# Turning U and V by VectorE in 32x32 blocks instead of by TensorE

## The chip, the cores and the metric

The kernel runs on one core of one Trainium2 chip. The metric is the device time of one execution in microseconds (us). Engines are named as in the profile: PE is the matmul engine TensorE (PEld its weight loads), DVE is VectorE, ACT is ScalarE, POOL is GpSimd, SP is SyncE, which here only issues transfers. Each engine works through its own queue of instructions in order; PSUM is the memory that PE writes, in 8 banks.

## The reference

A sequence `x` of 2048 tokens of width 576 goes through two layers. Each layer is a Fourier mix with a residual, then a two-layer perceptron with a residual.

```python
def _A_ref(x, dft_seq_re, dft_seq_im, dft_hid_re, dft_hid_im):
    a = jnp.einsum("bsd,ed->bse", x, dft_hid_re)
    b = jnp.einsum("bsd,ed->bse", x, dft_hid_im)
    y = jnp.einsum("ts,bse->bte", dft_seq_re, a) - jnp.einsum("ts,bse->bte", dft_seq_im, b)
    return y
def _B_ref(x, w1, b1, w2, b2):
    y = _layernorm(x, axis=-1)
    h = _gelu(jnp.einsum("bsd,df->bsf", y, w1) + b1)
    return jnp.einsum("bsf,fd->bsd", h, w2) + b2

x = x + _A_ref(_layernorm(x), ...)
x = x + _B_ref(_layernorm(x), ...)
...
```

The two DFT matrices of the sequence are 2048x2048, the two of the width 576x576; `w1` is 576x4608 and `w2` is 4608x576. All of it is fp32.

## The kernel before, in words

The order of the Fourier mix is turned round: first the sequence product, then the hidden one. For each of the 16 tiles of 128 output tokens, the sequence product gives U = Cr z and V = -(Ci z), 128 x 1152 numbers (`uv`), where z is the normalized input. Then the hidden product multiplies U and V by the 1152 x 576 matrix `dh` (the real part above the imaginary part) and adds the result to the residual `X`.

Each fp32 operand of a matmul is split in two parts, a high half that PE's fp32r mode can hold (an ACT copy, `high`, or the first line of `split`) and the rest (a DVE subtraction, `low`, or the second line of `split`). Each product takes three passes (`PASSES`: high x high, high x low, low x high). Big products are done with seven multiplications instead of eight (`ORDER` names the seven), which costs sums and differences on DVE and POOL.

**The sequence product** (`Sequence.run`, lines 693 to 737). The first two tiles are plain products, done together in `first_mms`, input block by input block, in all 8 banks; `first_post` (599) copies each tile's four banks with ACT into a buffer and stores it to DRAM (`uv_mid`) from ACT's queue. The other 14 tiles are 7 steps each, 98 in all, of 24 matmuls. At step n the program emits, in this order: loads of blocks of the DFT matrix as ring buffers come free (`load_c`, on SP), the low half for step n+2 (DVE, with differences that belong to it), the sums of the next tile if the step is number 2 of `ORDER`, the high half for step n+3 (ACT), the 24 matmuls, and `post` (668), which takes the step's bank. The last of a tile's seven, i = 4, ends in line 689 (DVE) and the store of the tile from SP (690). In layer 0 each step also advances the background work (`pump`), which makes the split parts of `w1` with ACT, DVE and POOL. The program order on each engine is the order of emission: nothing is reordered by a scheduler.

Before the first of the 98 steps stands what is left of `Sequence.fill` (lines 477 to 484): the low half of step 0 with its sums, the high halves of steps 1 and 2, the sums of the last input block on DVE and POOL (`right_sums`), their high and low halves (`high_sums`, `low_sums`). `first_post(0)` is emitted ahead of these, `first_post(1)` after step 1.

**The hidden product** (`Hidden`, and `hidden` from 868). It is done in two halves of 8 tiles. A tile's U and V are loaded from DRAM (`load_uv`, 832) into one of two slots. `turn` (845) puts the transpose into PSUM, because PE contracts over partitions: 9 PE transposes of 128x128 into two pairs of banks taken from a ring of four (`space`), then three splits out of PSUM (512, 512 and 128 columns). In the loop over tiles (988 to 1026) the turn of tile n+1 is emitted ahead of the 54 matmuls of tile n. Tile 0 of the first half is turned in the last steps of the sequence product (`begin`, n == 5, line 772); tile 0 of the second half is turned in the last outer products of the first half's perceptron (`steps`, line 799).

**The perceptron** (`mlp`) follows each half. The change doesn't touch it.

## Time and profile before

| what | value |
|---|---|
| median of 3 runs | 2691.88 us (2689.53 to 2692.5) |
| span of the profiled execution | 2687.7 us |
| mean granted TensorE clock | 0.999 |
| sequence product, layer 0 | to about 375 us |
| hidden product, first half, layer 0 | about 375 to 440 us |
| hidden product, second half, layer 0 | from about 875 us |
| sequence product, layer 1 | about 1345 to 1720 us |
| hidden products, layer 1 | from about 1720 us, and from about 2204 us |

The profile is one execution of the program. Its span is the time from the first to the last instruction; the timed runs also hold what lies around it. A row of the timeline has the start, the length, the engine, the line of the program, the operation, output and input by the program's names, the count of merged instructions, and in square brackets the idle time of the engine before it with what ended that. A row of a group (lines by form) has the busy time, the mean length in ns, and the idle time before with its causes. Line 205, 195, 198 and 201 are helpers (matmul, add, subtract, split); a row there is told apart by its shape. In the rows of stretches, each engine's busy time stands in the order PE, PEld, DVE, ACT, POOL, then the granted clock and the share and rate of the transfers.

### The profile page before, as it was taken

What the parts mean: (1) busy time and instruction counts of PE and PEld (TensorE: products, weight loads), DVE (VectorE), ACT (ScalarE), POOL (GpSimd) and SP (SyncE); (2) the same over time, 40 slices, a digit from 0 to 9 for tenths busy, and PEclk for the clock granted to TensorE, in tenths of its full rate; (3) what the DMA queues carried; (4) which work ended last, traced back from release to release, by engine and by line L of the source; (5) the groups of instructions that cost most, each with busy time, mean ns of one, the idle gap of its engine ahead of it and who ended that gap; (6) DMA issues with size and microseconds to landing.
All of it is one profiled execution on the core that took longest, in us unless ns stands there. A gap on an engine that the chain in (4) does not pass through costs nothing. (4 is left out here: it accounts for less than half of the span.)

```text
span 2687.7 us, 45270 instructions
## 1 busy us (share of the span) xinstructions
PE 2663.8 (99%) x17540; PEld 2498.7 (93%) x17540; DVE 1770.9 (66%) x2575; ACT 1101.4 (41%) x1837; POOL 791.3 (29%) x738
## 2 busy tenths in 40 slices
PE   9999999999999999999999999999999999999999
PEld 9999999888888988988899999999989899899998
DVE  8888866877777565556676666466555546655555
ACT  6555545544443343333354333343333324433332
POOL 6322234444443432222250000142222234322222
PEclk9999999999999999999999999999999999999999
DMA  5777775777778466676553333546666673666664
GB/s 190 253 259 245 243 264 186 261 265 273 262 267 305 148 187 195 191 221 208 161 202 130 122 123 124 191 145 193 193 194 196 191 274 115 206 194 194 193 194 153
DMA packets 209286, 544.92 MB, mean 203 GB/s; under 512 B 22048, under 2 KB 56864, under 8 KB 208928
## 3 DMA queue, kind: packets, MB, share of 16 engines
q1 hardware_dynamic: 195744, 511.94, 58.8%
q10 hardware_dynamic: 13328, 30.09, 2.9%
q8 instruction: 139, 2.28, 0.3%
q14 instruction: 75, 0.61, 0.1%
HBM read 429.87 MB, written 114.72 MB: 203 GB/s over the span
## 5 line engine op out<-in xcount | busy, mean ns | idle before, releaser
L205 PE MATMUL bank<-R 128*128 128x288 f32 (+2 forms) x16972 | 2607.8, 315 | 14.5 <-DVE A L195 5.6
L205 PEld LDWEIGHTS bank<-R 128*128 128x128 f32 x16972 | 2437.4, 188 | 176.0 <-DVE A L195 18.0
L195 DVE TENSOR_TENSOR A<-bank,A 128x576 f32<-128x576 f32 (+3 forms) x808 | 568.5, 710 | 536.5 <-PE bank L205 454.8
L198 POOL TENSOR_TENSOR R<-A,R 128x512 fp32r<-128x512 f32 (+1 forms) x286 | 373.2, 1315 | 903.9 <-ACT R L1230 864.4
L198 DVE TENSOR_TENSOR R<-A,R 128x1024 fp32r<-128x1024 f32 (+9 forms) x523 | 496.1, 972 | 56.0 <-ACT R L643 22.4
L195 POOL TENSOR_TENSOR A<-A 128x576 f32<-128x576 f32 (+2 forms) x102 | 138.1, 1358 | 564.9 <-ACT A L683 366.1
L1169 ACT ACTIVATE bank<-bank,b1t 128x512 f32<-128x512 f32 (+1 forms) x224 | 144.9, 647 | 369.1 <-DVE bank L195 242.5
L1230 ACT ACTIVATE R<-A 128x512 fp32r<-128x512 f32 x288 | 176.8, 629 | 271.8 <-DVE A L198 123.5
L198 POOL TENSOR_TENSOR A<-A 128x384 f32<-128x384 f32 (+3 forms) x156 | 197.3, 1267 | 246.2 <-DVE R L198 118.7
L643 ACT ACTIVATE R<-A 128x1024 fp32r<-128x1024 f32 x196 | 204.6, 1052 | 121.2 <-DVE A L198 98.2
L195 DVE TENSOR_TENSOR bank<-bank,A 128x512 f32<-128x512 f32 (+1 forms) x228 | 152.3, 670 | 143.4 <-PE bank L205 142.6
L198 DVE TENSOR_TENSOR R<-bank,R 128x512 fp32r<-128x512 f32 (+1 forms) x328 | 205.3, 640 | 51.5 <-ACT R L201 46.8
L198 DVE TENSOR_TENSOR A<-A 128x1024 f32<-128x1024 f32 (+3 forms) x134 | 140.9, 1058 | 4.5 <-DVE R L198 0.2
L1196 ACT ACTIVATE A<-bank 128x512 f32<-128x512 f32 (+1 forms) x76 | 43.7, 576 | 225.8 <-PE bank L205 225.8
L1230 ACT ACTIVATE R<-bank 128x512 fp32r<-128x512 f32 x216 | 121.4, 595 | 30.3 <-PE bank L205 30.3
L198 DVE TENSOR_TENSOR A<-bank,A 128x512 f32<-128x512 f32 x144 | 98.1, 681 | 0.0
L201 ACT ACTIVATE R<-bank 128x512 fp32r<-128x512 f32 (+1 forms) x112 | 49.4, 490 | 81.4 <-PE bank L855 75.2
L1169 ACT ACTIVATE A<-bank,b1t 128x512 f32<-128x512 f32 (+1 forms) x76 | 50.6, 666 | 66.6 <-DVE bank L195 66.6
L685 DVE SCALAR_TENSOR_TENSOR A<-A 128x288 f32<-128x288 f32 x28 | 16.0, 572 | 83.4 <-POOL A L195 83.4
L275 ACT ACTIVATE R<-A 128x256 fp32r<-128x256 f32 x126 | 51.9, 412 | 41.8 <-DMA A<-in_w 17.8
L249 ACT ACTIVATE A<-A,moments 128x576 f32<-128x576 f32 x58 | 48.6, 863 | 48.2 <-POOL moments L230 19.8
L276 ACT ACTIVATE R<-A,power,middle 128x128 fp32r<-128x128 f32 x126 | 60.8, 483 | 0.0
(66 smaller groups left out, 625.9 us busy)
## 6 DMA issues: line engine op xcount, KB each, us to landing
R<-w_parts SPq DMA_DIRECT2D x504, 320.0 KB, 3.4
R<-w_parts SPq DMA_DIRECT2D x189, 576.0 KB, 3.7
A<-in_cs SPq DMA_DIRECT2D x112, 512.0 KB, 4.0
w_parts<-R SPq DMA_DIRECT2D x63, 576.0 KB, 4.8
w_parts<-R ACTq DMA_DIRECT2D x81, 320.0 KB, 3.0
uv_mid<-A SPq DMA_DIRECT2D x28, 576.0 KB, 3.1
w_parts<-R SPq DMA_DIRECT2D x45, 320.0 KB, 4.3
A<-in_w SPq DMA_DIRECT2D x72, 192.0 KB, 4.6
```

The source lines that it names most:

```text
L195: engine.tensor_tensor(dst, a, b, op=op)
L198: engine.tensor_tensor(dst, a, b, op=OP.subtract)
L201: nc.scalar.activation(hi, src, AF.Copy)
L205: nc.tensor.matmul(o, a, b, start=start, stop=stop, skip_group_check=True)
L249: nc.scalar.activation(dst, src, AF.Identity, bias=mv[:, 4:5], scale=mv[:, 3:4])
L275: nc.scalar.activation(t[:, 1:4:2], src[:, 0:3:2], AF.Copy)
L276: nc.scalar.activation(t[:, 2], src[:, 1], AF.Identity, bias=power[:, 2:3], scale=middle)
L643: nc.scalar.activation(self.cells[t, i](2, NP, P)[:, 0], self.source(t, i), AF.Copy)
L685: nc.vector.scalar_tensor_tensor(uv[:, 1, 0], p7, -1.0, u, op0=OP.mult, op1=OP.subtract)
L1169: nc.scalar.activation(dst, src, AF.Gelu_apprx_tanh, bias=bias(f))
L1196: nc.scalar.activation(up, o, AF.Copy)
L1230: nc.scalar.activation(H[q, k](2, TC)[:, 0], src, AF.Copy)
```

## The change

DVE transposes each finished tile of U and V in place, block by block of 32x32 (one instruction over 128 x 1152), before it is stored. A 32x32 block then holds 32 of the 1152 columns in its rows, but still in the partitions of its 32 tokens. The load from DRAM moves the blocks to partitions by column group: four transfers, one for each 32 partitions, each of 32 partitions x 4 runs of 288 numbers. What lies in SBUF is then the whole transpose, with the columns in another order: partition 32c + d, chunk k holds column 288c + 32k + d. The rows of `dh` are put into the same order on the host. `turn` is then one split, an ACT copy and a DVE subtraction over 128 x 1152 that read the loaded tile with runs of 32 numbers, and no PSUM is used for it; `space` is no longer called there, so the other users of the ring of banks get other banks.

```diff
+    def turned(block):
+        nc.vector.transpose(block(2 * D), block(2 * D))
...
                     nc.scalar.activation(uv[:, i, 1 - j], banks[4 * (1 - t) + 2 * i + j][:, :DH], AF.Copy,
                                          scale=-1.0 if i else 1.0)
+            turned(out)
             nc.scalar.dma_start(uvd[t], out(2 * D))
...
                 nc.vector.scalar_tensor_tensor(uv[:, 1, 1], b, -1.0, u, op0=OP.mult, op1=OP.subtract)
+                turned(self.out)
                 dma(uvd[t], self.out(2 * D))
...
             self.uv[n] = self.uvs.take()
-            at = self.uv[n](2 * D)
-            dma(at.bitcast(F32) if self.half else at, uvd[8 * self.half + self.order[n]])
+            at = self.uv[n](4, DH)
+            src = uvd[8 * self.half + self.order[n]].rearrange("(q d) (c k) -> c d q k", q=4, c=4)
+            for c in range(4):
+                to = at[32 * c:32 * c + 32]
+                dma(to.bitcast(F32) if self.half else to, src[c])
...
-            v = self.uv[n](KH, P)
-            v = v.bitcast(F32) if self.half else v
+            v = self.uv[n](2 * D)
+            v = (v.bitcast(F32) if self.half else v).rearrange("p (q k t) -> p k q t", q=4, t=32)
             self.ut[n] = place or R.place(UT_AT[self.half][n % 2], 2 * KH * P)
-            o = self.ut[n](2, KH, P)
-            a, b = self.space(), self.space()
-            for k in range(KH):
-                at = (a, b)[k // 8][:, k // 4 % 2, k % 4 * P:(k % 4 + 1) * P]
-                nc.tensor.transpose(at, v[:, k], ident)
-            for k0, k1, at in ((0, 4, a[:, 0]), (4, 8, a[:, 1]), (8, 9, b[:, 0, 0:P])):
-                split(o[:, 0, k0:k1], o[:, 1, k0:k1], at.rearrange("p (k t) -> p k t", t=P))
-                yield
+            o = self.ut[n](2, KH, 4, 32)
+            split(o[:, 0], o[:, 1], v)
+            yield
             self.uvs.give(self.uv.pop(n))
...
-    dh = np.concatenate([dr.T, di.T], axis=0).reshape(KH, P, D)
+    dh = np.concatenate([dr.T, di.T], axis=0).reshape(4, KH, 32, D).transpose(1, 0, 2, 3).reshape(KH, P, D)
```

## The prediction

> **What bounds the kernel now.** I read the page's busy table first, then TensorE's timeline for its idle places, the rows of the transposes and of the splits by form, the timeline of DVE, ACT and SP round each place that gets new work, and the table of stretches.

> ```profile
> span 2687.7 us, 45270 instructions
> PE 2663.8 (99%) x17540; PEld 2498.7 (93%) x17540; DVE 1770.9 (66%) x2575; ACT 1101.4 (41%) x1837; POOL 791.3 (29%) x738
> ```

> TensorE (PE) is busy for 99% of the span, so whatever leaves its stream shortens the kernel, as long as nothing that PE waits for becomes later. The two questions are how much PE time the transposes take, and where VectorE (DVE), which gets new work, is already close behind PE. The profiled execution's span is 2687.7 us. The median of the three timed runs is 2691.9, so 4.2 us lie around the span, and I leave them alone.

> **What is removed from PE.** Line 855 makes 9 transposes per tile for 32 tiles:

> ```profile
> L855 PE MATMUL bank<-ident,A x144: 270/272/328, 371.9 to 1772.2; 128*128 128x128 f32 x144
> L855 PE MATMUL bank<-ident,R x144: 270/273/327, 864.7 to 2254.0; 128*128 128x128 f32 x144
>   DVE A L195: 0.9, 4
> ...
> 377.06 2.92 PE L205 MATMUL bank<-R 128*128 128x288 f32 x20 [0.36 <-DVE R L198]
> 393.16 1.15 PE L855 MATMUL bank<-ident,A 128*128 128x128 f32 x9
> 394.06 7.44 PE L205 MATMUL bank<-R 128*128 128x288 f32 x54
> 864.68 1.15 PE L855 MATMUL bank<-ident,R 128*128 128x128 f32 x9
> 868.25 3.93 PE L205 MATMUL bank<-R 128*128 128x288 f32 x28 [0.80 <-DVE A L195]
> 2197.77 6.68 PE L205 MATMUL bank<-R 128*128 128x288 f32 x48 [0.71 <-DVE A L195]
> ```

> One transpose lasts 272 ns, but they are pipelined: nine start at 393.16 and the next matmul starts at 394.06. The price is therefore 0.90 us per tile, not 9 x 0.272, and 32 x 0.90 = 28.8 us leave the stream. Four groups of waits hang on them. The transposes themselves waited 0.9 us in all for PSUM banks that DVE had not freed. Tile 1 waited 0.36 us at 377.06 for its split, which came behind its transposes. At 868.25 and 2197.77 the first turn of the second half ran inside the last outer products: ACT and DVE could split only after PE's transposes, DVE's add to X was queued behind that, and PE waited for the bank (0.80 and 0.71). The new split depends on a load that is long home and uses no PSUM, so all four should go: 2.8 us. Removed: 31.6 us.

> **What changes in the splits.**

> ```profile
> L198 DVE TENSOR_TENSOR R<-bank,R 128x512 fp32r<-128x512 f32 x292 | 197.6, 683 | 51.5 <-ACT R L201 46.8 <-ACT R L1230 4.2
> L198 DVE TENSOR_TENSOR R<-bank,R 128x128 fp32r<-128x128 f32 x32 | 9.0, 281 | 0.0
> L201 ACT ACTIVATE R<-bank 128x512 fp32r<-128x512 f32 x76 | 43.0, 587 | 81.4 <-PE bank L855 75.2 <-issue 6.2
> L201 ACT ACTIVATE R<-bank 128x128 fp32r<-128x128 f32 x32 | 8.7, 272 | 0.0
> L198 DVE TENSOR_TENSOR R<-A,R 128x1152 fp32r<-128x1152 f32 x16 | 21.6, 1352 | 3.8 <-ACT R L579 3.8
> L579 ACT ACTIVATE R<-A 128x1152 fp32r<-128x1152 f32 x16 | 18.5, 1158 | 6.8 <-POOL A L198 6.8
> ```

> Per tile ACT had 2 x 587 + 272 = 1446 ns and gets one instruction of 1158. DVE had 2 x 683 + 281 = 1647 and gets 1352. Both lie beside 7.3 us of matmuls of the tile before, so I count nothing for them.

> **What is added to DVE.** One in-place transpose of 128x1152 fp32 per tile, 32 in all. No DVE transpose is in the trace. The nearest row has the same size and two operands, 1352 ns, and successive DVE instructions start about 0.09 us before the last one ends, so it costs the queue 1.27 us. I take that. [...]

> [...]

> **Where DVE has no room: the start of each layer's sequence product.** `first_post(0)` puts its transpose into DVE's queue ahead of the low half of the first step, and it waits for four copies out of PSUM, hence for PE.

> ```profile
> 59.66 0.41 ACT L603 ACTIVATE A<-bank 128x288 f32<-128x288 f32 x1 [0.38 <-PE bank L205]
> ...
> 58.77 1.22 DVE L195 TENSOR_TENSOR A<-A 128x1024 f32<-128x1024 f32 x1
> 60.03 3.15 DVE L198 TENSOR_TENSOR A<-A 128x1024 f32<-128x1024 f32 x3
> 63.64 1.58 DVE L198 TENSOR_TENSOR R<-A,R 128x1024 fp32r<-128x1024 f32 x1 [0.46 <-ACT R L643]
> 67.11 2.49 DVE L198 TENSOR_TENSOR R<-A,R 128x1152 fp32r<-128x1152 f32 x2 [1.89 <-ACT R L579]
> ...
> 69.66 19.34 PE L205 MATMUL bank<-R 128*128 128x288 f32 x144 [0.25 <-DVE R L198]
> 89.54 282.48 PE L205 MATMUL bank<-R 128*128 128x288 f32 x2134 [0.54 <-DVE R L198]
> ...
> 1404.32 0.41 ACT L603 ACTIVATE A<-bank 128x288 f32<-128x288 f32 x1 [0.38 <-PE bank L205]
> 1410.67 0.41 ACT L675 ACTIVATE A<-bank 128x288 f32<-128x288 f32 x1 [0.24 <-PE bank L205]
> ...
> 1401.16 1.22 DVE L195 TENSOR_TENSOR A<-A 128x1024 f32<-128x1024 f32 x1
> 1409.52 2.50 DVE L198 TENSOR_TENSOR R<-A,R 128x1152 fp32r<-128x1152 f32 x2 [1.90 <-ACT R L579]
> ```

> Before, DVE did the first low half early and began the sums at 58.77. With the change the last copy ends at 60.07, the transpose starts at about 60.1, the first low half (1.13) follows 1.27 later, and the sums begin at 62.5: the chain moves by 3.8 us. It is a chain: sums and differences on DVE, the right sums on POOL, ACT's high half, DVE's low sums and the low half of the third step, which ends at 69.60, just when PE, already 0.25 late, takes it. So the whole 3.8 us reach PE, most of it as a wait of about 2.8 in the second step (whose low half moves from 65.2 to 69.0, wanted at about 66.2). In layer 1 the copy ends at 1404.73 and the sums move from 1401.16 to 1407.2, by 6.0. The chain's end moves from 1412.02 to 1418.0. PE finished step 0 at 1410.6, so it wants it at 1410.6 + 3.2 + 0.3 = 1414.1: 4.0 us late. ACT's store of U and V also waits for the transpose; behind it stands a high half that waits longer anyway. `first_post(1)` has a 1.9 us gap in DVE behind it. Cost: 7.8 us.

> **The other 28 transposes.**

> ```profile
> 90.00:350.00 260.00, 260.00 (x1968) 260.00 (x1967) 224.71 (x247) 151.13 (x272) 79.29 (x53) 1.00 0.73 251
> 1425.00:1700.00 275.00, 275.00 (x2082) 275.00 (x2081) 181.54 (x189) 107.02 (x137) 9.67 (x12) 1.00 0.35 119
> ...
> 132.12 0.45 DVE L689 SCALAR_TENSOR_TENSOR A<-bank,A 128x288 f32<-128x288 f32 x1
> 134.66 1.92 DVE L198 TENSOR_TENSOR A<-A 128x1024 f32<-128x1024 f32 x1
> 142.42 1.23 DVE L195 TENSOR_TENSOR A<-A 128x1024 f32<-128x1024 f32 x1 [2.27 <-DMA A<-in_cs]
> 144.82 2.82 DVE L198 TENSOR_TENSOR R<-A,R 128x1024 fp32r<-128x1024 f32 x3
> ...
> 136.64 0.33 SPq L192 DMA_DIRECT2D A<-in_cs  x1
> ...
> 1436.13 0.46 DVE L195 TENSOR_TENSOR A<-bank,A 128x288 f32<-128x288 f32 x1 [2.33 <-PE bank L205]
> ```

> DVE is busy 86% of the stretch in layer 0 (it also makes the weight parts) and 66% in layer 1. A tile takes 7 x 3.17 = 22.2 us. In layer 0 that leaves 3.0 us, but not all of it is free. The transpose sits behind line 689; the subtraction of 134.66 follows it, frees a block, SP loads into it (136.64), and the sums at 142.42 wait for that load, so DVE's 2.27 us gap does not absorb a later transpose. The low half after those sums ends at 146.04; PE's step starts at 69.66 + 24 x 3.174 + 0.54 = 146.4 and takes it two matmuls later: 0.6 us to spare, 1.27 needed. The same reckoning for the other tiles of layer 0 (the last apart, whose low halves wait for ACT) gives 0.6 to 2.4 to spare, some 19 us over 12 tiles, and less than 1.27 in three (0.85, 0.6, 0.7): 1.7 us of waits. In layer 1 DVE waits 2.33 us for PE (1436.13) a few instructions behind line 689, before any load is wanted, and that gap takes the transpose in: nothing. SP's store waits for the transpose too, and the block load queued behind it is the one just counted.

> **The loads.**

> ```profile
> L192 SPq DMA_DIRECT2D A<-uv_mid x16: 319/325/2116, 355.7 to 1754.8; - x16
> DMA to landing us min/median/max: 2.8/3.7/8.7
> ```

> Four transfers instead of one: SP issues for 1.3 us instead of 0.33, and the slot is freed by DVE's split, not by PE. Loads are issued more than one tile (7.3 us) ahead of their split, and the split another ahead of the matmuls. Cover: matmuls of two tiles; nothing counted. Without it, 1 us per tile would be 32.

> **Sum.** 31.6 - 7.8 - 1.7 = 22.1 us: a span of 2665.6, and 2691.9 - 22.1 = **2669.8 us**.

> **Rivals.** *The transpose is dear* (the slower side). With a queue price T, the two starts cost 2T + 5.2 and layer 0, from about 2.4 us, 12T - 19: together 14T - 13.8. It decides from T = 3.2, where this equals 31.6. [...] 0.06. *Twice the price*: T = 2.6 costs 22.6 and leaves 9.0, so 2683. 0.10. [...] 0.12. *Late loads*: four small transfers per tile hold the split back by about a microsecond per tile, which gives it all back: about 2692. It speaks against it that landing took 3.7. 0.05. *Slow clock after the start waits*:

> ```profile
> 1328.77 6.92 PE L205 MATMUL bank<-R 128*128 128x288 f32 x48 [2.02 <-DVE A L195]
> ```

> PE's longest idle time is 2.02 us, and the granted clock in the stretches above is 1.00. My wait of 2.8 would be the longest yet; if PE then ran one step at half pace in each layer, 3.2 us more each, 2676. [...] 0.07.

> **Numbers.** My forecast has 0.60. The range of 2662 to 2684 runs from the cheaper transpose to twice the price and leaves out the dear transpose, the late loads and part of the cheaper case, under 2 in 10. Measurement tells about 0.2% (5.4 us) from no change. Faster: 0.60 + 0.10 + 0.12 + 0.07 = 0.89, less 0.01 that I give to same, with the late loads: 0.06; slower 0.06.

> **What the new profile would show.** Line 855 gone; 32 DVE transposes near 1.35 us; PE idle of about 4 us in all near 66 to 73 and again near 1400, released by DVE's low halves; a few waits under a microsecond up to 350; matmuls of one hidden tile following the last without a break. DVE transposes over 2.5 us, or PE waiting on the split while `uv_mid` lands, would make it wrong.

## The result, and the profile after

The changed kernel takes 2699.65 us (median of 6 runs, 2696.38 to 2701.92), the kernel before 2690.74 beside it (6 runs, 2689.48 to 2692.5): ratio 1.0032, 95% interval 1.0022 to 1.0042. It is slower by 0.3%. The forecast was 2669.8 with a range of 2662 to 2684; it is wrong in sign and by 30 us. The profiled execution of the changed kernel is the longest of its six (2701.92 us), that of the kernel before one of its shortest (2689.53), so the two spans below differ by 12.4 us where the medians differ by 8.9.

The busy table of the page after:

```profile
span 2700.1 us, 44682 instructions
PE 2647.4 (98%) x17252; PEld 2479.5 (92%) x17252; DVE 1812.7 (67%) x2543; ACT 1096.6 (41%) x1773; POOL 811.8 (30%) x738
```

PE's idle time is span less busy: 23.9 us before, 52.7 after. The record of the granted clock has, apart from one at the very end of each program, seven spells of 3.41 us at half speed after and none before. Half of each is lost, 7 x 1.705 = 11.9 us, and that hides in PE's busy time. PE's work at full clock is therefore 2647.4 - 11.9 = 2635.5, that is 28.3 less than before. So the account is -28.3 of work, +28.8 of waiting, +11.9 of half clock: +12.4 of span. The work went as forecast; the waiting ate it. Where it is, PE's waits after (total us, times, longest) say:

```profile
PE bank L934 <- POOL A L917: 17.6, 8, 2.5
PE bank L208 <- DVE A L195: 6.7, 6, 2.6
PE bank L208 <- DVE R L198: 6.0, 10, 1.1
PE bank L208 <- ACT R L647: 2.8, 2, 1.4
PE bank L208 <- ACT A L685: 2.5, 1, 2.5
PE bank L208 <- DMA R<-w_parts: 2.1, 1, 2.1
```

The first line has no counterpart before: line 934 is PE's last four transposes in `turn_blocks`, which arrange the normalized result of a hidden product for the perceptron, and line 917 is POOL's copies of the last columns (`rests`), which they read. It happens twice in each of the four hidden products. Four of the seven spells lie behind these waits (at 447.0, 942.0, 1795.3 and 2256.1 us), the others behind the waits at 378, 1355 and 1426. The 5 us behind one of these waits, as a row of stretches:

```profile
446.00:451.00 5.00, 4.71 (x25) 4.71 (x26) 2.47 (x6) 3.52 (x5) 2.27 (x5) 0.66 0.17 67
```

The mean granted clock is 0.66: PE counts as busy for 4.71 of 5 us, and 1.7 us of that are lost. The groups by form, after:

```profile
L195 POOL TENSOR_TENSOR A<-A 128x576 f32<-128x576 f32 x56 | 98.7, 1767 | 91.8 <-ACT A L252 49.5 <-DVE A L195 41.8
L205 DVE STREAM_TRANSPOSE A<-A 128x1152 f32<-128x1152 f32 x32 | 44.1, 1378 | 8.3 <-ACT A L606 7.4
L198 DVE TENSOR_TENSOR R<-A,R 128x1152 fp32r<-128x1152 f32 x32 | 43.2, 1351 | 12.6 <-ACT R L201 8.7 <-ACT R L582 3.8
L201 ACT ACTIVATE R<-A 128x1152 fp32r<-128x1152 f32 x16 | 18.6, 1160 | 17.3 <-PE bank L208 15.2 <-DMA A<-uv_mid 2.0
```

The transpose (1378 ns) and the splits (1351 and 1160) cost what was forecast. POOL's add of 128x576 became slower without being touched; before, its row was:

```profile
L195 POOL TENSOR_TENSOR A<-A 128x576 f32<-128x576 f32 x56 | 87.9, 1575 | 77.1 <-DVE A L195 41.2 <-ACT A L249 33.7 <-DMA A<-x_mid 1.8
```

**The chain beside the hidden product.** The timeline of the kernel before, from the last transposes of one pair of tiles to those of the next pair:

```profile
419.91 0.60 PE L931 MATMUL bank<-ident,A 128*96 128x128 f32 x4
...
421.27 7.45 PE L205 MATMUL bank<-R 128*128 128x288 f32 x54
...
424.80 1.86 DVE L198 TENSOR_TENSOR R<-A,R 32x256 fp32r<-32x256 f32 x4
...
426.82 4.27 POOL L198 TENSOR_TENSOR A<-A 128x384 f32<-128x384 f32 x4 [1.95 <-DVE R L198]
...
432.52 0.58 ACT L201 ACTIVATE R<-bank 128x512 fp32r<-128x512 f32 x1
433.00 0.86 ACT L249 ACTIVATE A<-A,moments 128x576 f32<-128x576 f32 x1
...
433.93 1.93 POOL L195 TENSOR_TENSOR A<-A 128x576 f32<-128x576 f32 x1 [1.79 <-ACT A L249]
435.81 0.75 POOL L914 COPY A<-A 128x128 f32<-128x128 f32 x3
...
437.61 0.60 PE L931 MATMUL bank<-ident,A 128*96 128x128 f32 x4
```

DVE's lows release POOL's four differences; behind these, in POOL's queue, stand the layer norm's moments, then ACT normalizes (line 249), POOL adds b2 and copies, and PE transposes. The copies end at 436.56, PE comes at 437.61: 1.05 us to spare. The same places after:

```profile
428.11 0.64 PE L934 MATMUL bank<-ident,A 128*96 128x128 f32 x4 [2.50 <-POOL A L917]
...
428.51 14.62 PE L208 MATMUL bank<-R 128*128 128x288 f32 x108
...
430.68 4.37 DVE L198 TENSOR_TENSOR R<-A,R 128x1152 fp32r<-128x1152 f32 x5 [2.63 <-ACT R L201]
...
431.48 1.85 POOL L195 TENSOR_TENSOR A<-A 128x576 f32<-128x576 f32 x1 [2.25 <-ACT A L252]
...
435.22 4.30 POOL L198 TENSOR_TENSOR A<-A 128x384 f32<-128x384 f32 x4 [1.89 <-DVE R L198]
...
440.95 1.15 ACT L201 ACTIVATE R<-A 128x1152 fp32r<-128x1152 f32 x1
442.00 0.86 ACT L252 ACTIVATE A<-A,moments 128x576 f32<-128x576 f32 x1
442.94 2.59 POOL L195 TENSOR_TENSOR A<-A 128x576 f32<-128x576 f32 x1 [2.36 <-ACT A L252]
...
445.47 0.76 POOL L917 COPY A<-A 128x128 f32<-128x128 f32 x3
...
446.29 0.64 PE L934 MATMUL bank<-ident,A 128*96 128x128 f32 x4 [2.28 <-POOL A L917]
```

Counted from the tile's first matmul, PE is at its transposes after 16.34 us before and 15.50 after (446.29 - 2.28 - 428.51): 0.84 less, the transposes taken out between. The chain ends after 15.29 us before and 17.72 after: 2.43 more. The differences start 1.16 later (6.71 instead of 5.55 after the tile's start; four lows of 1.86 us have become some 3.0, beside POOL's add). From their start to the normalize's end it is 0.60 more (7.64 instead of 7.04): ACT's split in front of it is one piece of 1.15, no longer a first piece of 0.58. The add takes 2.59 instead of 1.93, beside DVE's lows. 1.05 - 0.84 - 2.43 = -2.22, and PE waits 2.28.

That count begins at the tile's first matmul and so leaves out one of the two turns beside which the chain runs: the chain begins with the transposes of the pair before, at 419.91 and at 428.11. From there PE is at the next transposes after 17.70 us before and 15.90 after, 1.80 less, two turns of 0.90. The chain ends after 16.65 and 18.12, 1.47 more: the differences start 0.20 later, up to the normalize's end it is 0.60, the add 0.66. 1.05 - 1.80 - 1.47 is -2.22 again. Of the two, each would have made a wait by itself, by this count 0.75 us from the shorter tiles and 0.42 from the longer chain.

### The profile page after: what moved, and what is told of

The parts are those of the page before. It is cut to its first block, busy times and chain, and to the rows that moved or that the text cites. A ratio compares the mean times of both kernels' runs of the same rounds, so it can differ in the third digit from the quotient of the medians.

```text
span 2700.1 us, 44682 instructions
## 1 busy us (share of the span) xinstructions
PE 2647.4 (98%) x17252; PEld 2479.5 (92%) x17252; DVE 1812.7 (67%) x2543; ACT 1096.6 (41%) x1773; POOL 811.8 (30%) x738
## 5 line engine op out<-in xcount | busy, mean ns | idle before, releaser
L195 DVE TENSOR_TENSOR A<-bank,A 128x576 f32<-128x576 f32 (+3 forms) x808 | 568.3, 710 | 521.2 <-PE bank L208 425.9
L198 POOL TENSOR_TENSOR R<-A,R 128x512 fp32r<-128x512 f32 (+1 forms) x286 | 373.5, 1317 | 904.1 <-ACT R L1233 865.4
L198 DVE TENSOR_TENSOR R<-A,R 128x1024 fp32r<-128x1024 f32 (+10 forms) x539 | 521.4, 990 | 86.0 <-ACT R L944 33.6
L195 POOL TENSOR_TENSOR A<-A 128x576 f32<-128x576 f32 (+2 forms) x102 | 152.1, 1494 | 572.8 <-ACT A L687 351.6
L198 POOL TENSOR_TENSOR A<-A 128x384 f32<-128x384 f32 (+3 forms) x156 | 193.5, 1243 | 262.9 <-DVE R L198 101.9
L195 DVE TENSOR_TENSOR bank<-bank,A 128x512 f32<-128x512 f32 (+1 forms) x228 | 152.2, 670 | 143.8 <-PE bank L208 142.9
L198 DVE TENSOR_TENSOR R<-bank,R 128x512 fp32r<-128x512 f32 x232 | 156.3, 676 | 4.8 <-ACT R L1233 4.2
L198 DVE TENSOR_TENSOR A<-A 128x1024 f32<-128x1024 f32 (+3 forms) x134 | 140.2, 1053 | 4.5
L198 DVE TENSOR_TENSOR A<-bank,A 128x512 f32<-128x512 f32 x144 | 98.0, 681 | 0.0
L689 DVE SCALAR_TENSOR_TENSOR A<-A 128x288 f32<-128x288 f32 x28 | 16.0, 571 | 73.6 <-POOL A L195 73.6
L944 ACT ACTIVATE R<-A 128x768 fp32r<-128x768 f32 (+2 forms) x36 | 32.8, 945 | 56.1 <-POOL A L198 56.0
```

Source lines behind the costliest of these rows:

```text
L195: engine.tensor_tensor(dst, a, b, op=op)
L198: engine.tensor_tensor(dst, a, b, op=OP.subtract)
L689: nc.vector.scalar_tensor_tensor(uv[:, 1, 0], p7, -1.0, u, op0=OP.mult, op1=OP.subtract)
L944: nc.scalar.activation(y[:, i, 0:3, at], x, AF.Copy)
```

## The experiments

Medians are of the timed runs; the kernel before ran beside each, at 2691.98 beside e1 to e4 and at 2690.77 to 2690.96 beside the others. "Less" and "more" without another name are against the changed kernel's 2699.65.

**e1_parts_later.** Theory: ACT's queue. `turn_parts` is emitted a tile later, behind the drain of the turn and the layer norm.

```diff
-            if n in (3, 5):
-                turn_parts((n - 3) // 2)
...
             if n:
                 drain(turn(n + 1), *ln)
+            if n in (4, 6):
+                turn_parts((n - 4) // 2)
```

> The changed kernel, with the last parts of a tile (turn_parts, an ACT copy that waits for four POOL differences) put behind the split and the normalization in the next tile's turn. Theory A, ACT's queue: the copy for which ACT waits stands ahead of the new split and of the normalization, whose result POOL must copy before TensorE may turn the blocks; so all eight waits for POOL (17.6 us in the changed kernel's trace) go, and with them the four half-clock spells behind them (4 x 1.7). About 2675 us, 0.994 of the kernel before. Rival B, POOL itself: POOL's own work (differences, the slower add, the copies) is what comes late; over 10 us of the waits stay, and the time stays within 5 us of 2700.

2701.8 us (ratio 1.0034, 1.0023 to 1.0045); the waits for POOL were 19.7. Nothing gained: at one of the places ACT's normalize then waited 5.07 us for POOL's moments (the layer norm's small sums), which stood behind POOL's differences (5.30 us). ACT's queue alone is not the cause.

**e2_norm_first.** The normalize ahead of the split in ACT's queue.

```diff
-                drain(turn(n + 1), *ln)
+                drain(*ln, turn(n + 1))
```

> The changed kernel, with the normalization of the tile before emitted ahead of the split of the next tile, not behind it. Theory A: normalization starts 1.2 us earlier in each tile, so each wait for POOL falls from 2.5 to about 1.3 and some of the half-clock spells go: 2683 to 2692 us. Rival C, the shorter tile alone decides and ACT's order in a tile doesn't matter: the waits stay at 2.3 to 2.5, and the time at 2700.

2706.78 us (1.0047, 1.003 to 1.0064), waits for POOL 22.0, longest 3.4. Worse: the normalize was not moved forward, because ACT's high half ahead of it waits for POOL's differences anyway (6.98 us there), and the split came later.

**e3_ballast.** Eight transposes per tile are put back on PE, from the loaded tile into a bank that nobody reads. Work is added, nothing is left out.

```diff
             o = self.ut[n](2, KH, 4, 32)
+            a = self.space()
+            u = self.uv[n](KH, P)
+            u = u.bitcast(F32) if self.half else u
+            for k in range(8):
+                nc.tensor.transpose(a[:, k // 4, k % 4 * P:(k % 4 + 1) * P], u[:, k], ident)
```

> The changed kernel with eight useless TensorE transposes per turn, whose result nobody reads: TensorE gets about 0.8 us of work per tile back, everything else stays. If the waits for POOL come because a tile became 0.9 us shorter (two tiles lie between the differences and the turning of the blocks), each falls from 2.5 to about 0.9 and the half-clock spells behind them go: the 25 us of ballast are mostly paid by 13 us of waits and 7 us of clock, 2703 to 2708 us. If they come from the longer split on ACT or from POOL slowed by VectorE, they stay, and the time is near 2725.

2706.88 us (1.0053, 1.0038 to 1.0068). Its busy table and first wait:

```profile
PE 2668.3 (99%) x17508; PEld 2499.4 (92%) x17508; DVE 1813.6 (67%) x2543; ACT 1096.9 (41%) x1773; POOL 811.2 (30%) x738
```

```profile
PE bank L939 <- POOL A L922: 5.9, 8, 1.0
```

With the tile near its old length the waits fall from 17.6 to 5.9 and the spells behind them vanish (two are left, at the layer starts: 3.4 us lost). PE's work at full clock is 2668.3 - 3.4 = 2664.9, 29.4 more than in the changed kernel, and the span is only 4.2 longer (2704.3), the median 7.2. So at least three quarters of what leaves PE is not seen in the time, because something else is then late. Beside the kernel before, e3 has the same work on PE (2664.9 and 2663.8) and is 14.9 us slower: about that much comes from what the change adds, without the shorter tile. The waits for POOL that are left, 0.7 us each, are near what the longer chain alone would make by the count above (0.4), with the ninth transpose still missing in each of two turns (0.2).

**e4_late_turn.** At the layer starts the first tile's transpose and store go behind the preparation of the 98 steps (store still on ACT).

```diff
-            turned(out)
-            nc.scalar.dma_start(uvd[t], out(2 * D))
+
+        def first_store(self, t, out):
+            turned(out)
+            nc.scalar.dma_start(uvd[t], out(2 * D))
...
+            self.first_store(0, outs[0])
             outs.append(
```

> The changed kernel, with the VectorE transpose and the store of the first tile of each layer put behind the rest of the preparation, so that VectorE's low half of the first step no longer stands behind TensorE. My prediction's account of the two starts (transpose queued ahead of the chain): the waits at both starts (2.9 and 2.5 us in the changed kernel's trace) and one half-clock spell (1.7) go, 7 us: about 2692.5. Rival: the chain is as long from another cause (DMA, POOL), and 2 us or less are won.

2691.04 us (0.9995, 0.9986 to 1.0005): 8.6 less, as expected (9.8 if each is set against the kernel before beside it). Layer 1's start waits nowhere, where 2.5 us of waits and a spell were. Layer 0's start is not cured: ACT's queue now waits behind the store (2.50 us at 71.86, with a spell), and at 251 us e4 is no further than the changed kernel (251.56 beside 251.20). The rest of e4's gain is at places that it does not touch; its waits for POOL, for one, are 14.9 us instead of 17.6.

**e5_uv_later.** The second load of U and V is issued at step n == 5 of `begin`, not at n == 0.

```diff
                 self.load_uv(0)
-                self.load_uv(1)
+            if n == 5:
+                self.load_uv(1)
```

> The changed kernel, with the load of the second tile of U and V (four of the eight transfers that SP issues at the start of the last sequence tile) issued five steps later. Theory: those eight transfers hold up the load of raw weights behind them on SP, ACT waits for it (9.1 us), and TensorE for ACT's copy (2.5 us, with 1.7 us of half clock). With four transfers the weights come about 3 us sooner: the wait at 378 us goes, 2 to 5 us in all, about 2695.5 us. Rival: the weights are late from the memory's load at that place, and nothing changes.

2694.27 us (1.0015, 1.0006 to 1.0025): 5.4 less, as expected, but for the most part not at the place that its theory names. There the changed kernel has this chain: eight transfers hold SP for 5.83 us, the raw weight rows issued behind them land late, ACT waits for one, and the copy that frees PE's bank stands behind it.

```profile
364.02 5.83 SPq L192 DMA_DIRECT2D A<-uv_mid  x8
...
374.82 0.42 ACT L278 ACTIVATE R<-A 128x256 fp32r<-128x256 f32 x1 [9.13 <-DMA A<-in_w]
...
378.16 8.72 PE L208 MATMUL bank<-R 128*128 128x288 f32 x52 [2.52 <-ACT A L685]
...
387.55 21.32 PE L208 MATMUL bank<-R 128*128 128x288 f32 x158 [0.66 <-DVE R L198]
```

In e5 the weight row lands sooner (ACT starts at 372.60, not 374.82) and the wait of 2.52 falls to 0.87, which bears out the queue as its cause. But the second wait, for the low half of tile 0, which stands on DVE behind parts of weight rows, grows by as much:

```profile
385.35 22.84 PE L208 MATMUL bank<-R 128*128 128x288 f32 x158 [2.24 <-DVE R L198]
```

The two are 3.11 us together, where they were 3.18, and one half-clock spell is still there, now behind the second. e5's trace has four spells instead of seven, 5.1 us, with those missing at other places, and the wait at the second half's start is 1.42 instead of 2.64.

**f1_sums_on_dve, and f2_before_sums as its control.** POOL's differences go to DVE, in the changed kernel and in the kernel before.

```diff
-            g = nc.gpsimd if j < 2 else nc.vector
+            g = nc.vector
```

> The changed kernel, with the four differences of turn_sums on VectorE for every tile (before: on POOL for the first two). Theory B, POOL's queue: these differences (4.3 to 5.3 us) hold back the next tile's normalization statistics, its add and the copies that TensorE waits for; the tile that became 0.9 us shorter no longer covers them. All eight waits for POOL (17.6 us) fall below 1 us each and most of the four half-clock spells behind them (6.8 us) go: 2675 to 2682 us. Rival: the wait is for the add and the copies, slowed by VectorE's reading of SBUF beside them; then VectorE's extra work leaves 1 to 2.5 us per wait, and the time stays above 2690.

> The kernel before, with the same move of the four differences to VectorE. It had no wait for POOL there, so theory B has nothing to win: 2691 us, within 0.1% of the kernel before. If the move is a gain of its own, whatever the transposes do, it is faster by 5 us or more.

f1: 2691.2 us (1.0003, 0.9994 to 1.0012), 8.5 less; the waits for POOL's copies halve to 8.8, and 3.5 us of waits for ACT's normalize appear. f2: 2690.97 (1.0, 0.999 to 1.0009). So POOL's differences are a link of the late chain, and before they were no bound.

**f3_all.** f1 and e5 together with e4's late transpose, whose store goes to SP.

> The changed kernel with all three cures: the differences on VectorE, the first tile's transpose and store behind the preparation (the store on SP, so that ACT doesn't wait for it), and the second load of U and V later. If the three causes are what took the 28.8 us of TensorE time back, they add up: 24 + 8 + 3 us below the changed kernel, about 2664 us, 0.990 of the kernel before. If other work is next on the path, 2675 us or more.

2685.3 us (0.9981, 0.9972 to 0.999), faster than before, but the causes did not add up: 22.5 us were cured one by one, 14.4 together. One reason stands in the trace: at the beginning of the hidden products f3 still waits 0.71 and 2.23 us, with a spell, so e5's 5.4 us were not that place's. PE's waits:

```profile
PE bank L939 <- POOL A L922: 9.7, 8, 1.3
PE bank L208 <- DVE R L198: 6.9, 8, 2.2
...
PE bank L936 <- ACT A L252: 3.8, 7, 0.7
```

**g1_rests, g3_begin, g5_all, and g4_before_cures as control.** g1 is f3 with the copies of `rests` on DVE. g3 is g1 with the first tile's split ahead of three weight rows' parts in `begin`. g5 is g3 with e1's move. g4 is the kernel before with differences and copies on DVE.

```diff
-                    nc.gpsimd.tensor_copy(es(7, 3, 32)[:, :4, r], v[:, 0:4, 2 * P:])
+                    nc.vector.tensor_copy(es(7, 3, 32)[:, :4, r], v[:, 0:4, 2 * P:])
...
-            for k in ((), (), (), (), (0, 1, 2), (3, 4, 5), (6, 7, 8))[n]:
-                self.high_d(k)
-                self.low_d(k)
             if n == 5:
                 drain(self.turn(0, Block(R, self.first_ut, 2 * KH * P)))
                 self.load_uv(2)
+            for k in ((), (), (), (), (0, 1, 2), (3, 4, 5), (6, 7, 8))[n]:
+                self.high_d(k)
+                self.low_d(k)
```

> The kernel with the three cures (differences on VectorE, late transpose at the layer starts, second load of U and V later) took 2685.3 us and still had 9.7 us of waits for the last pieces' copies on GpSimd, 3.8 us for ScalarE's normalise, and three half-clock spells (5.1 us). Here those copies (0.77 us alone, more beside VectorE) go to VectorE for three of the four rests; nothing else changes. Theory A, that GpSimd's end of the chain (its add, then its copies) is what TensorE waits for: the copies drop out, the 9.7 fall to about 2 to 4 us, two spells with them: about 2675. Rival, that the chain is late before GpSimd's copies (its moments, then ScalarE's normalise, end late whoever copies): the waits only change their releaser, and the time stays within 2682 to 2687.

> As g1_rests, and at the beginning of the hidden products the first tile's split is emitted ahead of the high and low parts of three weight rows, not behind them. TensorE waited 2.23 us at 384.5 for VectorE's low part there, with a half-clock spell of 1.7 us behind it. Theory: the order in VectorE's and ScalarE's queues is that wait's cause, and it goes: 3 to 4 us less than g1_rests. Rival: the raw weight row lands late behind the eight transfers of U and V, so that whoever is second waits for it: same time as g1_rests, the wait with another releaser.

> As g3_begin, and the drain of the next tile's pieces goes ahead of ScalarE's and VectorE's share of the sums (turn_parts a step later), the move that alone, with GpSimd's differences still in the chain, moved the waits from GpSimd to ScalarE and left the time as it was. Theory A (the chain's length from blocks to rests decides): starting the sums later makes it no shorter; same as g3_begin within 3 us. Rival (queue order on ScalarE decides now that GpSimd is short): 3 to 6 us less than g3_begin. If the causes found add up, the better of the two is at about 2668 to 2672, near the prediction on record.

> The kernel before with the differences and the rests' copies on VectorE instead of GpSimd: its TensorE never waited for GpSimd. Theory (the chain had slack there and was no bound): no change, 2689 to 2693. Rival (moving this work is a gain of its own, whatever the transposes do): faster by over 5 us, which would make part of the cured kernels' gain no cure of the change.

g1: 2695.49 us (1.0012, 1.0003 to 1.0021), 10 us more than f3 where 10 less were expected. DVE's timeline in g1:

```profile
422.71 1.71 DVE L922 COPY A<-A 128x128 f32<-128x128 f32 x3 [0.98 <-ACT A L252]
...
424.34 0.75 DVE L195 TENSOR_TENSOR A<-bank,A 128x576 f32<-128x576 f32 x1
```

The copies are not shorter on DVE (1.71 us for three), and DVE stands still for 0.98 us until ACT's normalize is done; its add to X, the head of the next tile's chain, stands behind both. The wait moved to ACT's normalize (10.4 us), 6.2 us stayed at the copies, and g1's trace loses 11.9 us to half clock, f3's 5.1. g3: 2691.52 (1.0004, 0.9995 to 1.0012), 4.0 less than g1, as its theory had it, and the two waits at the beginning are 0.32 and 0.27 us; but the runs of the two kernels overlap (2686.1 to 2696.93 and 2689.13 to 2700.74). g5: 2703.35 (1.0043, 1.0031 to 1.0055), 11.8 more than g3, outside both expectations: the waits for DVE's copies were 22.5. g4: 2690.14 (0.9994, 0.9986 to 1.0003), no change.

**h1_blocks, h2_blocks_f3, h3_blocks_begin, and h5_before_blocks as control.** The transposes that wait are moved 3.2 us later in PE's order: in the changed kernel, in f3, in f3 with the order of `begin` as in g3, and in the kernel before.

```diff
-            if n >= 2 and n % 2 == 0:
+            if n == NP - 2:
                 turn_blocks(n // 2 - 1)
...
-                if n in (3, 5) and k == 2:
+                if n in (3, 5) and k == 4:
+                    turn_blocks((n - 3) // 2)
+                if n in (3, 5) and k == 6:
                     turn_sums((n - 3) // 2)
```

> The changed kernel with one move: TensorE's transposes of the blocks of the first two pairs of tiles stand behind the fourth of nine steps of the next tile's product (about 3.2 us later) instead of ahead of it, and the sums of these blocks two steps behind them; no link of the chain that they wait for gets shorter. Theory A (the chain from the first product's end to the copies has one tile of time, the change made the tile 0.9 us shorter, and the chain, 2.5 us too long, is what PE waits for): the 17.6 us of waits and the four half-clock spells behind them (6.8 us) go, 2699.65 - 24.4 = about 2675. Rival (the engines beside TensorE are short of throughput in these tiles, and whatever is moved, PE waits for the next thing): the waits come back at the banks of the products or at the next blocks, and the time stays over 2690.

> The kernel with the three cures (2685.3 us) and the same move. Theory A: its remaining 9.7 + 3.8 us of waits and the two spells behind them (3.4 us) go: about 2668, by chance the forecast. Rival: over 2680, with waits at another place of the same tiles.

> As h2_blocks_f3, and at the beginning of the hidden products the first tile's split is emitted ahead of the high and low parts of three weight rows. In the two kernels with and without that order this was worth 4 us (2695.5 to 2691.5): about 2665. If that was chance of the half-clock spells alone: same as h2_blocks_f3 within 2 us.

> The kernel before with the same move. It had no wait at these transposes. Theory A: no change, 2689 to 2692. Rival (the move is a gain of its own, whatever the change does): faster by over 3 us.

2709.39 us (1.0069, 1.0056 to 1.0081), 2699.74 (1.0035, 1.0023 to 1.0047), 2698.01 (1.0029, 1.0019 to 1.0039), and 2695.54 for the kernel before (1.0016, 1.0007 to 1.0025). The theory's numbers failed in all four, and in h1 and h2 the rival's held; in the kernel before, where these transposes had not waited, the move costs 4.6 us and brings 3.0 us of waits for POOL's copies. h3 is only 1.7 us under h2, inside the 2 us that its expectation gives to chance, so what the order of `begin` is worth stays open. In h1:

```profile
416.24 1.86 DVE L198 TENSOR_TENSOR R<-A,R 32x256 fp32r<-32x256 f32 x4 [4.16 <-ACT R L944]
418.01 0.75 DVE L195 TENSOR_TENSOR A<-bank,A 128x576 f32<-128x576 f32 x1
...
425.24 0.80 PE L208 MATMUL bank<-R 128*128 128x288 f32 x4 [0.95 <-ACT R L201]
```

The lows of the sums came later with their blocks, and DVE waited 4.16 us for ACT's highs with its add to X queued behind; PE then waited for the next tile's split (0.95, then 1.38). So the move is no clean test: it gave the chain's end more time and its beginning a wait.

**i1_rests_first, i2_all.** The chain itself is made shorter: POOL's add of b2, which the copies don't need, goes behind them. i1 is the changed kernel with this alone; i2 is f3 with it and with g3's order of `begin` (copies on POOL).

```diff
                 normalize(z, tile_x, mv)
-                add(nc.gpsimd, tile_x, tile_x, b2t(2, DH))
+                if n % 2 == 0:
+                    add(nc.gpsimd, tile_x, tile_x, b2t(2, DH))
...
                 rests(n // 2 - 1)
+                tile_x = xv[:, :, order[n - 1]]
+                add(nc.gpsimd, tile_x, tile_x, b2t(2, DH))
```

> The changed kernel with one move: for the second tile of each of the first three pairs, GpSimd's add of b2 to X stands behind the copies of the last pieces, which do not need it, and not ahead of them. Theory A (the chain that ends in these copies is what TensorE waits for, and the tile's 0.9 us were its slack): the add's 2.59 us leave the chain; the copies then run beside VectorE's lows, up to 1.1 us slower than alone, so the waits of 17.6 us fall to between 0 and 8, and the four half-clock spells (6.8 us) go: 2676 to 2683, about 2680. Rival (short queues everywhere, whatever is moved PE waits for the next thing, as in the moves of the blocks): over 2690.

> The three cures (2685.3 us), the first tile's split ahead of the weight parts at the beginning, and this move. If the causes add up: 9.7 us of waits fall to 1 to 4, two spells behind them go (3.4), and the beginning gives 3.9: 2669 to 2674. If the waits come back elsewhere, as in the moves of the blocks: over 2680.

i1: 2682.8 us (0.997, 0.9958 to 0.9981), 16.85 less than the changed kernel, as theory A had it. Its timeline and first wait:

```profile
439.90 0.85 ACT L252 ACTIVATE A<-A,moments 128x576 f32<-128x576 f32 x1
...
440.82 1.97 POOL L918 COPY A<-A 128x128 f32<-128x128 f32 x3 [2.34 <-ACT A L252]
442.76 1.42 POOL L195 TENSOR_TENSOR A<-A 128x576 f32<-128x576 f32 x1
442.85 0.64 PE L935 MATMUL bank<-ident,A 128*96 128x128 f32 x4 [0.91 <-POOL A L918]
```

```profile
PE bank L935 <- POOL A L918: 8.3, 8, 1.2
```

The add's 2.59 us leave the chain, the copies take 1.97 instead of 0.76 beside DVE's lows, so it ends 1.38 earlier, and PE's wait falls from 2.28 to 0.91, by 1.37. All four spells of the hidden products are gone.

i2: 2674.98 us (5 runs, 2672.0 to 2676.86; 0.994, 0.9927 to 0.9954). It is the fastest of all, faster than both kernels and 1 us above what was expected if the causes add up. No run has i1's move or the order of `begin` in the kernel before, so how much of the 15.8 us by which i2 is under it would be gained there too is not shown.

```profile
PE 2639.0 (99%) x17252; PEld 2469.5 (92%) x17252; DVE 1830.3 (68%) x2575; ACT 1097.5 (41%) x1773; POOL 785.4 (29%) x706
```

```profile
PE bank L208 <- DVE R L198: 6.0, 10, 1.5
PE bank L208 <- DVE A L195: 5.2, 5, 2.0
PE bank L937 <- ACT A L252: 4.9, 8, 0.7
```

The wait for POOL is gone from the list; 4.9 us of waits for ACT's normalize remain of the chain, and one half-clock spell. The two waits at the beginning are 0.41 and 0.25 us.

## Why the prediction was wrong

**Right.** The transposes' price on PE (28.8 forecast, 28.3 measured), the transpose on DVE (1352 taken, 1378 measured), and the layer starts: 7.8 forecast; the waits are 1.42, 1.07, 0.34 and 0.34 against 0.25 in layer 0 and 1.42 and 1.08 in layer 1, 5.4 in all, with one half-clock spell 7.1. They came as a wait of 1.42 for ACT's high half and one of 1.07 or 1.08 for DVE's low half, not as one of 2.8. e4 shows the cause in layer 1 (nothing waits there any more); in layer 0 no run took the waits away, and that e4's 8.6 us in all are near the 7.8 is luck. The other tiles of layer 0 cost 0.6, not 1.7. The range's lower end stands on a cheaper transpose, which no run shows: the 32 took 1378 ns each on average.

**The step that failed: "Both lie beside 7.3 us of matmuls of the tile before, so I count nothing for them."** I looked at whether the split is done in time for the next tile and never at what else lives in that time. Taking 0.9 us per tile out of PE takes as much from every chain that runs beside the tile; the chain that ends in POOL's copies runs beside two turns, lost 1.80 us, and had 1.05 to spare. The change also lengthened it, by 1.47: ACT's split comes in one piece ahead of the normalize, and the low half now reads two operands from SBUF (`R<-A,R`) where it had read one and a bank. e3 gave PE most of the time back, and the waits for POOL fell from 17.6 to 5.9 us; i1 took 2.59 us out of the chain, and they fell to 8.3, with 16.85 us of the time. POOL's adds and copies are long where lows of this kind run beside them (the add 2.59 us at 442.94, the copies 1.97 at 440.82 in i1, against 0.76 without lows beside them), and the add at 423.44 in the kernel before, beside a low that read a bank, took 1.44; that the second operand from SBUF is the cause is not shown, because no run changed it alone. Both rows were in the profile before: the copies' end and PE's transposes stood a microsecond apart.

**The loads, "nothing counted".** I asked whether U and V land in time, and they do. What landed late was the weight row issued behind them on the same queue; the place was the one where two tiles' loads are issued together. With a half-clock spell it cost 4.9 us against the forecast (2.52 and 0.66 of waits, and 1.7). e5 shows the queue as the cause of the first wait, but its 5.4 us are not a measure of the place, where another wait took the first one's. The 0.36 at 377.06, by the way, was tile 0's third pass waiting for its own low half, not tile 1, so the change could not take it away: it is the 0.66 at 387.55. The rival of late loads was also added up wrongly: a microsecond per tile is 32 us, hence 2702 and not 2692, which would need 0.7.

**The waits that should vanish.** The one of 0.71 in layer 1 is gone; the one of 0.80 at the second half's start became 2.64. In the rows of the changed kernel it isn't the split that stands ahead of it:

```profile
872.53 0.68 ACT L1107 ACTIVATE R<-A 128x576 fp32r<-128x576 f32 x1 [5.80 <-DMA w_parts<-R]
...
873.25 0.76 DVE L198 TENSOR_TENSOR R<-A,R 128x576 fp32r<-128x576 f32 x1 [3.70 <-ACT R L1107]
...
875.48 28.18 PE L208 MATMUL bank<-R 128*128 128x288 f32 x210 [2.64 <-DVE A L195]
```

DVE's adds to X follow the low half of 873.25, which waited 3.70 us for ACT's part of a weight row, and ACT waited 5.80 us for a store of such parts. SP's queue is late there too: its loads of `in_x`, ahead of those stores, start 0.39 us after PE's row of 849.99 before, and 2.63 us after the same row at 859.91 in the changed kernel, behind more transfers of U and V. That the transfers are the cause is likely but not shown; no run changed them alone.

**The slow clock** had 0.07, tied to the waits at the starts. It took 11.9 us, most of it behind waits that I did not foresee. The forecast's 3.2 us for a step at half pace was an assumption that no run shows: in the changed kernel's trace the spells followed waits of 2.13 to 2.52 us (1.42 and 1.08 together in one case), and each cost 1.7 us.

The gap of 34.5 us between the forecast's span (2665.6) and the measured one (2700.1; between the medians it is 29.9) is then: hidden products 17.6 + 4 x 1.7 = 24.4; their beginning 4.9; the second half's start 2.6; the wait at 1355 for `w_parts`, 1.1 longer and with a spell, 2.8; the layer starts -0.7; layer 0's other tiles -1.1; in all 32.9, and 1.6 unassigned. The runs show the first (e3, f1, i1) and layer 1's start (e4) as causes. The beginning and the second half's start are read from the rows alone, as far as their size goes; the wait at 1355 is open, and so is what is left of the difference between 22.5 and 14.4 us in f3.

## What to carry to other kernels

An engine that is 99% busy hides the slack of every chain beside it: before taking time out of it, list for each of its instructions per tile how long its input had been ready, and follow the chain behind that input back to its start. What was ready for less than the time removed along the whole chain (here two turns, 1.80 us), plus what the change adds to the chain (1.47), becomes the new wait. When such a chain is late, take out of it what its end does not need (here an add, 16.85 us); moving a link to another engine's queue helped once (f1) and once put it ahead of something else that was due (g1). Follow the other instructions on the queue that gets more transfers, not only the transfers themselves. When an experiment gives the time that its theory named, look in its trace whether it gave it at the place that the theory named (e4 and e5 for the most part did not).
